# Thirty transfers of 2-byte rows on ScalarE's queue, in a decode kernel that streams a key/value cache

## The chip, the cores and the metric

The kernel runs on one core of a Trainium2 chip. The metric is the device time of one execution in microseconds (us). The kernel before took 1295.4 us (median of two runs, 1295.17 and 1295.63). A separate execution was profiled, and all rows of the trace come from it.

The engines are named as in the profile: PE is TensorE (PEld its weight loads), DVE is VectorE, ACT is ScalarE, POOL is GpSimd, SP is SyncE. A name with a q behind it (ACTq, SPq) is that engine's instruction sequencer. The core has 16 DMA engines, which carry the transfers that SP and ACT issue.

## The reference

One token per sequence (batch 8) goes through attention over a cache of 4096 positions (32 heads of 128) and, beside it, through an MLP; a sigmoid gate mixes the two.

```
q = (x @ wq) -> 8 x 32 heads x 1 x 128
p = softmax(q . k_cache / sqrt(128))        # k_cache: 8 x 32 x 4096 x 128, bf16
a = (p @ v_cache) -> 8 x 1 x 4096, @ wo     # v_cache: the same shape; wo: 4096 x 576
h = gelu(layernorm(x) @ w1 + b1)            # w1: 576 x 4608
b = h @ w2 + b2
g = sigmoid(sum(x * gate_w))
out = g * a + (1 - g) * b                   # 8 x 1 x 576
```

The two caches are 268 MB each, read once. They are nearly all of the 557 MB that the kernel moves.

## The kernel before

The work is cut into 32 groups, n = 0 to 31. A group is one sequence of the batch and 8 heads. Its keys are 8.4 MB and lie on 128 partitions (16 partitions for a head, 256 positions on each, so 64 KB per partition); its values are as large. The groups are gone through in order:

- **Scores.** `mult(n, c)` (line 501, DVE) multiplies a chunk of 32 positions by the query, which `q_group` (line 476, ACT) copied into `q_n`. PE sums the products over the 128 numbers of a head with an identity matrix (lines 512 and 183), and `reduce` (line 524, DVE) ends the sum. There are 8 chunks in a group.
- **Softmax.** DVE finds the maximum (lines 541 to 549), ACT takes the exponential (line 550), DVE writes the probabilities `P` (line 553).
- **Values.** One group behind, `pv(n - 1)` (line 565, PE) multiplies the probabilities by the values; `evict(n - 1)` (line 577, ACT) copies the sum out of PSUM into `O_sb`; `gather(n - 1)` (line 582, PE) keeps each head's own part; `norm(n - 1)` (lines 587 and 588, DVE) divides by the sum of the exponentials; `put` (line 481, ACT) stores the result.

All loads of the caches are issued by SP. `load_k(n + 1)` (line 329) waits until the first half of the keys of group n has been multiplied. `load_v(n)` (line 340) waits until `pv(n - 1)` has read the one buffer of values. Small loads go through a helper `load` (its DMA is line 288), each with a semaphore of its own; ACT issues eleven of these: `x`, `gate_w`, `b1` at the start, then `g4` (four, from the tile `stat` in SBUF to the tile `g4` in SBUF, 8 rows of 8 bytes each, after the MLP's first part), and `b2` (four of 8 rows of 288 bytes, near the end). At the end it issues one half of the output.

An engine runs its instructions in the order in which the program's text puts them on its list: what stands later in ACT's list starts after what stands earlier.

**The end.** The values of the last group come in four parts (`V_LAST`: 128, 64, 32 and 32 positions), so that the work can follow the transfers closely. `pv` takes the first two parts, `evict(last)` and `gather(last)` follow, and `pv_turned` (line 776) adds the third and the fourth part in another layout. `preset` (line 759) lays the MLP's part under the result; then come `norm_turned` (line 786), `to_rows_last` (lines 724, 710 and 730), `a_proj` (line 768, the product with `wo`, whose last rows land in pieces), two copies out of PSUM (lines 866 and 867) and two output transfers (line 871), one from SP and one from ACT. SP then waits for both to land, which ends the program.

`ident` is the 128 x 128 identity, made at the start by GpSimd (`c_id`).

Of the kernel before, what the change touches and what calls it, by code (L numbers as in the profile page):

```python
# [9 lines left out]
BF16 = mybir.dt.bfloat16  # L10
# [31 lines left out]
class Stream:  # L42
# [11 lines left out]
    def op(self, engine, fn, waits=(), dma=None, side=0):  # L54

        rec = [fn, [w for w in waits if w is not None], None, dma, (engine, side)]
        self.ops[engine].append(rec)
        if dma is not None:
            return ("dma", *dma)
        return ("op", engine, rec)  # L60
# [84 lines left out]
def bass_gated_mix__mha_block_cached__mixer_channel_mlp__decode_kernel(  # L145
# [16 lines left out]
    sb = nc.alloc_sbuf_tensor  # L162
    S = Stream(nc)
    op = S.op

    def aside(engine, fn, waits=()):
        return op(engine, fn, waits, side=1)

    def pstride(t):
        return t[tuple([slice(None)] * len(t.shape))].ap[0][0]  # L170
# [67 lines left out]
    G8 = sb("G8", [128, B], F32)  # L238
    sel_f = sb("sel_f", [128, 2, 2, 32], F32)
    O_l = sb("O_l", [128, HB], BF16)  # L240
    g4 = sb("g4", [128, 2], F32)
    ident = sb("ident", [128, 128], BF16)
    ones = sb("ones", [128, 128], F32)
# [43 lines left out]
    def load(engine, dst, src, name, waits=()):  # L287
        return op(engine, lambda e: e.dma_start(dst, src), waits, dma=(nc.alloc_semaphore(name), 16))  # L288
# [36 lines left out]
    def load_k(n):  # L325
        nK[0] += 1
        waits = [k_done[0, 1]] if n == 1 else [k_done[n - 1, k_order(n - 1)[0]], st["p_up"]]
        dst = view(KR, k_base(n), [128, NTT, DH])
        t = op("sync", lambda e: e.dma_start(dst, kv_src(A_k_cache, n)), waits, dma=(sK, 16 * nK[0]))
        k_land[n, 0] = k_land[n, 1] = t  # L330
# [5 lines left out]
    def load_v(n, t0=0, t1=NTT, waits=()):  # L336
        nV[0] += 1
        src = kv_src(A_v_cache, n)[:, t0:t1, :]
        dst = VB[:, t0:t1, :]
        t = op("sync", lambda e: e.dma_start(dst, src), [*waits, v_done.get(n - 1)], dma=(sV, 16 * nV[0]))  # L340
        v_land[n] = t
# [4 lines left out]
    v_part = []  # L346
# [18 lines left out]
    def memset(engine, ap, value):  # L365
# [3 lines left out]
    c_id = op("gpsimd", lambda e: e.affine_select(out=ident[:], in_=ident[:], compare_op=ALU.not_equal, fill=1.0,  # L369
                                                  base=0, pattern=[[-1, 128]], channel_multiplier=1), [c_id0])  # L370
# [74 lines left out]
    for half in range(2):  # L445
        for h in range(4):
            for kt in range(NKT):
                o = tr_ps[half][32 * h:32 * h + B, :]
                at = (kt * SK + half * (SK // 2) if kt < NKF else NKF * SK) + h * DH
# [14 lines left out]
    def q_of(b):  # L464
        for i in range(2):
            t = aside("tensor", lambda e, i=i: e.matmul(  # L466
                qb_ps[64 * i:64 * i + 64, :], lhsT=Sel[:, b, :],
                rhs=bass.AP(tensor=Q4, offset=i * DH, ap=[[pstride(Q4), 128], [2 * DH, NHG], [1, DH]]),
                start=True, stop=True), [*a_Q, c_Sel, a_qb.get(b - 1)] if i == 0 else ())
        a_qb[b] = aside("scalar", lambda e: e.activation(out=q_bc[:, b, :], in_=qb_ps[:, :], func=ACT.Copy), [t])  # L470
# [3 lines left out]
    def q_group(n):  # L474
        hg, b = divmod(n, B)
        a_q[n] = aside("scalar", lambda e: e.activation(out=q_n[:, :], in_=q_bc[:, b, hg * DH:(hg + 1) * DH], func=ACT.Copy),  # L476
                    [a_qb[b], v_mult.get((n - 1, NC - 1))])
# [50 lines left out]
    def scores(n, between):  # L528

        mult(n, 0)  # L530
        between(0)
        mult(n, 1)
        between(1)
        for c in range(NC):
            reduce(n, c)
            if c + 2 < NC:
                mult(n, c + 2)
                between(c + 2)
# [21 lines left out]
    def pv(n, land, t0, t1):  # L560
# [7 lines left out]
                start=(tq < 4), stop=(tq >= (NTT if n < last else T_TURN) // TQ - 4)), w)  # L568
        v_done[n] = p_pv[n]

    def total(n):
        p_z[n] = op("tensor", lambda e: e.matmul(  # L572
            oz_ps[:, HB:2 * HB], lhsT=ones[:, :], rhs=rs[:, :], start=True, stop=True),
            [v_rs[n], v_norm.get(n - 1), c_ones])
# [73 lines left out]
    def batch_rows(t, n, i):  # L648

        p = pstride(t)  # L650
        return bass.AP(tensor=t, offset=i * 32 * p, ap=[[p, B], [1, n]])
# [8 lines left out]
    def down_proj(j0, j1):  # L660
        for jt in range(j0, j1):
            st["p_down"] = quarters(hT_sb, NJ, jt, w2_sb[:, jt, :], jt == 0, jt == NJ - 1,
                                    [st["ld_w2"], st["v_h"], c_yps] if jt == 0 else (),
                                    op if jt in (j0, NJ - 1) else aside)
            st.setdefault("p_down0", st["p_down"])

    def b_out():
        st["a_bx"] = aside("scalar", lambda e: e.activation(
            out=bmg_sb[0:QP, :], in_=y_ps[0:QP, 0:QN], func=ACT.Copy), [st["p_down0"], st["p_down"]])
# [9 lines left out]
    def load_wo():  # L679

        g = H_AHEAD // HB
        st["ld_wo"] = load("sync", wo_sb[:, 0:H_AHEAD, :].rearrange("p (g r) n -> p g (r n)", g=g),
                           A_wo[0:H_AHEAD * DH, :].rearrange("(g p r) n -> p g (r n)", g=g, r=RD), "ld_wo", [k_done[last - 1, 1]])
# [96 lines left out]
    def recip(n):  # L780
        t = op("vector", lambda e: e.reciprocal(out=rz[:, :], in_=oz_ps[:, HB:2 * HB]), [p_z[n]])
        v_rz[n] = op("vector", lambda e: e.tensor_scalar(
            out=rz[:, :], in0=rz[:, :], scalar1=G8[:, n % B:n % B + 1], scalar2=None, op0=ALU.mult), [t, st["a_G8"]])
# [9 lines left out]
    for n in range(NG):  # L793
        for e, (first, turn, _) in LOOP.items():
            if n >= first and (n - first) % turn == 0:
                S.marks.setdefault(e, []).append(len(S.ops[e]))

        def between(c, n=n):
            if n == 0 and c + 1 < B:
                q_of(c + 1)  # L800

        scores(n, between)
        if n < last:
            q_group(n + 1)
            load_k(n + 1)
        if n == 0:
            load_v(0, 0, V_AHEAD, [p_Q])
            g_diag = op("gpsimd", lambda e: e.tensor_scalar(
                out=stat[:, 16:16 + B], in0=ident[0:B, 0:B], scalar1=stat[:, G_COL:G_COL + 1], scalar2=None, op0=ALU.mult), [a_g, c_id])
            t = aside("tensor", lambda e: e.matmul(oz_ps[:, 0:B], lhsT=ones[0:B, :], rhs=stat[:, 16:16 + B], start=True, stop=True),  # L810
                      [g_diag, c_ones])
            st["a_G8"] = aside("scalar", lambda e: e.activation(out=G8[:, :], in_=oz_ps[:, 0:B], func=ACT.Copy), [t])
            up_proj()
            softmax(0)
            act_h()
            c_selO = op("vector", lambda e: e.tensor_reduce(
                out=selO[:].rearrange("p t h -> p h t"),
                in_=bass.AP(tensor=ident, offset=0, ap=[[pstride(ident), 128], [TQ, HB], [1, TQ], [32, 4]]),
                axis=AX.X, op=ALU.add), [c_id])
            v_omg = op("vector", lambda e: e.tensor_scalar(out=stat[:, OMG_COL:OMG_COL + 1], in0=stat[:, G_COL:G_COL + 1],  # L820
                                                           scalar1=-1.0, scalar2=1.0, op0=ALU.mult, op1=ALU.add), [a_g, st["p_up"]])
            st["a_g4"] = a_g4 = [load("scalar", batch_rows(g4, 2, i), stat[:, G_COL:G_COL + 2], f"ld_g4{i}", [v_omg, c_g4])
                    for i in range(4)]
            down_proj(0, NJ)
            b_out()
            load_v(0, V_AHEAD, NTT, [st["p_down"]])
            continue
        if n == last - 1:
            load_wo()
        total(n - 1)  # L830
        if n == last:
            to_rows_spread(range(NHG - 1))
        pv(n - 1, v_land[n - 1], 0, NTT)
        evict(n - 1)
        gather(n - 1, oz_ps[:, 0:HB])
        if n == last:
            S.marks["tensor"].append(len(S.ops["tensor"]))
        if n < last:
            load_v(n)
        softmax(n)  # L840
        norm(n - 1)
        if n == last:
            S.marks["vector"].append(len(S.ops["vector"]))
            to_rows_spread((NHG - 1,))
            to_rows()
        if n == last - 4:
            load_b2()
            b_gate()
    load_v_last(last)
    load_wo_last()  # L850
    total(last)
    a_proj_ahead()
    recip(last)
    for i in range(2):
        pv(last, v_part[i][2], *v_part[i][:2])
    evict(last)
# [12 lines left out]
    for i, e in enumerate(("sync", "scalar")):  # L869
        half = bass.AP(tensor=out_flat.tensor, offset=out_flat.offset + i * 2 * QN, ap=[[D, B], [1, 2 * QN]])  # L870
        ld_out = op(e, lambda e, i=i, half=half: e.dma_start(half, out_sb[32 * i:32 * i + B, :]), t, dma=(s_out, 16 * (i + 1)))
    S.ops["sync"].append([lambda e: None, [ld_out], None, None, None])


    S.resolve()
# [39 lines left out]
```

## Time and profile before

| what | value |
|---|---|
| median of two runs | 1295.4 us |
| the profiled execution's own time | 1295.31 us |
| its span, first to last instruction | 1293.2 us |
| DVE busy | 852.2 us (66%) |
| PE busy | 736.9 us (57%) |
| ACT busy | 73.7 us (6%) |
| moved by DMA | 557.08 MB, 431 GB/s over the span |
| packets of SP's and ACT's queues together (q1 and q10) | 11520 and 320 |

Busy time of an engine counts its compute instructions alone: the time that a sequencer spends on issuing a DMA is not in it. A DMA's row in the timeline is that issue; the transfer itself runs later on the 16 DMA engines. A time in a timeline is counted from the start of the span; the span plus 2.1 us is the execution's own time.

### The profile page before, as it was taken

To read this page: it belongs to the slowest core of one execution; us is meant where nothing else is said; L and a number is where in the kernel's file an instruction comes from. 1 tells how busy PE (TensorE), PEld (TensorE's weight loads), DVE (VectorE), ACT (ScalarE), POOL (GpSimd) and SP (SyncE) were. 2 spreads that over 40 slices of the span, in tenths; PEclk is the share of its full clock that TensorE was granted. 3 is DMA by queue.
4 is the path that set the end of the run, shared out by engine and by line. 5 is a ranking of instruction groups with operands and counts; after the bars stand their busy time and mean duration, and the time that the engine had idled before them with its cause. 6 is when DMAs were issued, how large, how long until landed. Compare 5 with 4: busy or idle time off the path is not lost.

```text
span 1293.2 us, 11048 instructions
## 1 busy us (share of the span) xinstructions
PE 736.9 (57%) x4888; PEld 142.9 (11%) x3096; DVE 852.2 (66%) x1078; ACT 73.7 (6%) x167; POOL 13.0 (1%) x26
## 2 busy tenths in 40 slices
PE   3745566455557555556555556555556555556556
PEld 0211111011111011111011111001111001111003
DVE  3646667766667766667766667766668766667763
ACT  3300000000000000000000000000000000000001
POOL 0100000000000000000000000000000000000001
PEclk8978888777898787898778888877898787799778
DMA  9999999999999999999999999999999999999998
GB/s 406 426 447 424 428 444 428 438 434 430 444 426 428 444 428 426 444 430 438 432 430 444 426 428 444 428 430 440 430 440 432 428 444 426 428 444 428 430 434 358
DMA packets 11848, 557.08 MB, mean 431 GB/s; under 512 B 1568, under 2 KB 1728, under 8 KB 2240
## 3 DMA queue, kind: packets, MB, share of 16 engines
q1 hardware_dynamic: 11520, 556.93, 99.7%
q10 hardware_dynamic: 320, 0.04, 0.0%
q8 instruction: 5, 0.08, 0.0%
q14 instruction: 3, 0.02, 0.0%
HBM read 556.96 MB, written 0.01 MB: 431 GB/s over the span
## 4 chain that ended last, share of the span: by engine, by line
DMA 67%; DVE 18%; PE 9%; issue 4%; DVEq 1%; SPq 0%
DMA KR<-in_A_k_cache_dram 65%; DVE p L501 15%; PE psb L183 8%; DVE s_sb L524 2%; DMA KR<-in_A_wo_dram 2%; PE psb L512 2%; DVEq L524 0%; DVEq L137 0%; SPq L288 0%; PE psb L768 0%; PE psb L466 0%; DVE p L866 0%; DVEq L501 0%
## 5 line engine op out<-in xcount | busy, mean ns | idle before, releaser
L501 DVE TENSOR_TENSOR p<-KR,q_n 128x4096 bf16<-128x4096 bf16 x256 | 582.1, 2284 | 211.1 <-DMA KR<-in_A_k_cache_dram 211.1
L183 PE MATMUL psb<-p,ident 128*128 128x512 bf16 x1792 | 491.1, 420 | 0.0
L512 PE MATMUL psb<-p,ident 128*128 128x512 bf16 x256 | 112.5, 440 | 505.9 <-DVE p L501 505.9
L524 DVE TENSOR_REDUCE s_sb<-psb 128x512 f32 (+1 forms) x256 | 175.7, 686 | 109.4 <-PE psb L183 62.8
L512 PEld LDWEIGHTS psb<-p,ident 128*128 128x128 bf16 x256 | 26.5, 103 | 965.2 <-DVE p L501 964.5
L565 PE MATMUL psb<-VB,P 128*32 128x512 bf16 x1984 | 112.7, 380 | 0.0
L553 DVE TENSOR_SCALAR P<-E,own 128x256 bf16<-128x256 bf16 x256 | 53.1, 283 | 87.4 <-ACT E L550 87.4
L476 ACT ACTIVATE q_n<-q_bc 128x128 bf16<-128x128 bf16 x32 | 9.9, 309 | 873.2 <-DVE p L501 873.2
L565 PEld LDWEIGHTS psb<-VB,P 128*32 128x32 bf16 x1984 | 50.0, 97 | 48.0
L582 PE MATMUL psb<-selO,O_sb 128*128 128x8 f32 x256 | 33.9, 259 | 22.5 <-ACT O_sb L577 22.5
L582 PEld LDWEIGHTS psb<-selO,O_sb 128*128 128x128 f32 x256 | 31.0, 191 | 38.3 <-ACT O_sb L577 38.3
L577 ACT ACTIVATE O_sb<-psb 128x512 f32<-128x512 f32 x32 | 19.1, 597 | 196.8 <-PE psb L565 196.8
L572 PEld LDWEIGHTS psb<-rs,ones 128*128 128x128 f32 x64 | 12.1, 190 | 46.6 <-issue 44.4
L550 ACT ACTIVATE E<-s_sb,mD 128x256 bf16<-128x256 f32 x32 | 16.0, 499 | 0.0
L541 DVE TENSOR_REDUCE mA<-s_sb 128x1 f32<-128x256 f32 x32 | 13.4, 420 | 1.1
L481 ACT ACTIVATE OT_sb<-O_n,G 128x8 bf16<-128x8 f32 x31 | 9.3, 300 | 84.3 <-DVE O_n L588 84.3
L556 DVE TENSOR_REDUCE es<-E 128x1 f32<-128x256 bf16 x32 | 13.2, 413 | 0.0
L672 POOL TENSOR_TENSOR Q<-Q,b 104x144 f32<-104x144 f32 x1 | 0.7, 742 | 1073.9 <-DMA b<-in_B_b_dram 1073.9
L572 PE MATMUL psb<-rs,ones 128*128 128x8 f32 x64 | 9.2, 216 | 1.3 <-DVE O_n L588 1.3
L557 DVE TENSOR_SCALAR rs<-own,es 128x8 f32<-128x8 f32 x32 | 7.4, 231 | 1.1
L643 PE MATMUL psb<-VB,hT_sb 128*8 128x144 bf16 x144 | 4.5, 324 | 5.5 <-POOL hT_sb L633 5.5
L549 DVE STREAM_TRANSPOSE mD<-mC 128x32 f32<-128x32 f32 x32 | 6.8, 213 | 1.1
(97 smaller groups left out, 130.9 us busy)
## 6 DMA issues: line engine op xcount, KB each, us to landing
KR<-in_A_k_cache_dram SPq DMA_DIRECT2D x2, 4096.0 KB, 27.1
VB<-in_A_v_cache_dram SPq DMA_DIRECT2D x1, 5376.0 KB, 28.9
VB<-in_B_w_dram SPq DMA_DIRECT2D x1, 5184.0 KB, 40.5
KR<-in_B_w_dram SPq DMA_DIRECT2D x1, 4608.0 KB, 43.5
VB<-in_A_wq_dram SPq DMA_DIRECT2D x1, 4096.0 KB, 12.4
KR<-in_A_v_cache_dram SPq DMA_DIRECT2D x1, 4096.0 KB, 22.3
VB<-in_A_v_cache_dram SPq DMA_DIRECT2D x1, 2816.0 KB, 38.2
KR<-in_A_wo_dram SPq DMA_DIRECT2D x1, 2304.0 KB, 20.7
```

The costliest lines, as they stand in the source:

```text
L183: return e.add_instruction(mybir.InstMatmult(name=nc.get_next_instruction_name(), engine=mybir.EngineType.PE, ins=[e.lower_ap(rhs), e.lowe ...
L501: v_mult[n, c] = op("vector", lambda e: e.tensor_tensor(out=p1[:, par, :, :], in0=k_of(), in1=qb, op=ALU.mult), [k_land[n, s], a_q[n], p_s ...
L512: fn = lambda e, r=r: e.matmul(tr_ps[par][:, :], lhsT=ident[:, :], rhs=r, start=True, stop=False)
L524: v_red[n, c] = op("vector", lambda e: e.tensor_reduce(out=s_of(), in_=tr_ps[par][:, :].rearrange("p (t c) -> p t c", c=CH), axis=AX.X, op ...
L541: t = op("vector", lambda e: e.tensor_reduce(out=mA[:, 0:1], in_=s_sb[:, :], axis=AX.X, op=ALU.max), [v_red[n, NC - 1], c_mA])
L550: a_exp[n] = op("scalar", lambda e: e.activation(out=E[:, :], in_=s_sb[:, :], func=ACT.Exp, bias=mD[:, 0:1], scale=1.0), [v_nm[n], v_P.get ...
L553: v_P[n] = op("vector", lambda e, h=h: e.tensor_scalar(out=P[:, :, h, :], in0=E[:, :].rearrange("p (q t) -> p q t", t=TQ), scalar1=own[:, ...
L556: t = op("vector", lambda e: e.tensor_reduce(out=es[:, :], in_=E[:, :], axis=AX.X, op=ALU.add), [a_exp[n]])
L565: p_pv[n] = op("tensor", lambda e, o=o, tq=tq, at=at, v=v: e.matmul(o, lhsT=P[:, tq, :, :].rearrange("p h t -> p (h t)"), rhs=v.rearrange( ...
L572: p_z[n] = op("tensor", lambda e: e.matmul(oz_ps[:, HB:2 * HB], lhsT=ones[:, :], rhs=rs[:, :], start=True, stop=True), [v_rs[n], v_norm.ge ...
L577: a_ev[n] = op("scalar", lambda e: e.activation(out=O_sb[:].rearrange("p t d -> p (t d)"), in_=o_ps[n // last][:, :], func=ACT.Copy), [p_p ...
L582: p_oz[n] = op("tensor", lambda e, tt=tt: e.matmul(o, lhsT=O_sb[:, tt, :], rhs=selO[:, tt, :], start=(tt == 0), stop=(tt == TQ - 1 and stop)),
```

## The change

A new tile `rows_to` (128 partitions x 30 numbers of 2 bytes) is written by 30 DMAs and read by nothing. Each copies a piece of the first column of the identity: 15 rows of 2 bytes, then 14, and so on down to 1, each into a column of its own, each with a semaphore of its own. ACT issues all of them. The first set stands in group n = 2, after `q_group(3)` and `load_k(3)` and ahead of `total(1)`, `pv(1)` and `evict(1)`; it waits for `c_id`. The second set stands behind `recip(last)` and ahead of the last group's `pv` and `evict(last)`; its first transfer waits for the landing of the third part of the last group's values (`v_part[2][2]`). At the very end SP waits for all 30 semaphores beside the output's.

```diff
+    rows_to = sb("rows_to", [128, 30], BF16)
...
+    tags = []
+
+    def rows_1_to_15(name, at, waits):
+
+        for k in range(15, 0, -1):
+            tags.append(load("scalar", rows_to[0:k, at + k - 1:at + k], ident[0:k, 0:1], f"{name}{k}", [*waits, c_id] if k == 15 else ()))
...
+        if n == 2:
+            rows_1_to_15("ld_r", 0, ())
         if n == last - 1:
             load_wo()
         total(n - 1)
...
     recip(last)
+    rows_1_to_15("ld_e", 15, [v_part[2][2]])
     for i in range(2):
         pv(last, v_part[i][2], *v_part[i][:2])
     evict(last)
...
-    S.ops["sync"].append([lambda e: None, [ld_out], None, None, None])
+    S.ops["sync"].append([lambda e: None, [ld_out, *tags], None, None, None])
```

## The prediction

> **What bounds the kernel now.** I read the page first: its span, the queues, the chain.
>
> ```profile
> span 1293.2 us, 11048 instructions
> GB/s 406 426 447 424 428 444 428 438 434 430 444 426 428 444 428 426 444 430 438 432 430 444 426 428 444 428 430 440 430 440 432 428 444 426 428 444 428 430 434 358
> q1 hardware_dynamic: 11520, 556.93, 99.7%
> q10 hardware_dynamic: 320, 0.04, 0.0%
> DMA 67%; DVE 18%; PE 9%; issue 4%; DVEq 1%; SPq 0%
> ```
>
> SP's queue (q1) keeps the 16 DMA engines busy for 99.7% of the span; ACT's queue (q10) moves almost nothing. Next the windows, whose last three columns are the granted clock, the DMA share and GB/s.
>
> ```profile
> 118.31:1240.71 1122.40, 638.74 (x4002) 109.89 (x2378) 765.18 (x958) 46.44 (x116) 1.39 (x2) 0.84 1.00 433
> 118.31:157.01 38.70, 21.59 (x138) 3.78 (x82) 26.38 (x33) 1.60 (x4) 0.00 (x0) 0.85 0.99 430
> 157.01:195.72 38.71, 22.70 (x138) 3.80 (x82) 26.39 (x34) 1.60 (x4) 0.00 (x0) 0.81 1.01 437
> ```
>
> A group takes 38.70 us because its 16.8 MB take that at 433 GB/s. So in the long middle only the stream of loads counts, and an engine may be late as long as no load is issued too late. At the end the stream runs dry, and there the order of the compute engines sets the time. The change has one set of transfers in each place.
>
> **What one issue costs ACT.** Timeline rows of ACT (start, length) and the groups of line 288 (shortest, median, longest ns):
>
> ```profile
> 1.68 0.37 ACTq L288 DMA_DIRECT2D b_sb<-in_B_b_dram  x1
> 2.08 1.28 ACT L379 ACT_TABLE_LOAD   x1 [2.08 <-issue]
> ...
> 63.24 2.74 ACTq L288 DMA_DIRECT2D g<-stat  x4
> ...
> 1118.58 1.32 ACTq L288 DMA_DIRECT2D b<-in_B_b_dram  x4
> ...
> L288 ACTq DMA_DIRECT2D g<-stat x4: 632/638/732, 63.2 to 65.3; - x4
> L288 ACTq DMA_DIRECT2D b<-in_B_b_dram x4: 284/310/319, 1118.6 to 1119.6; - x4
> ```
>
> ACT's first own operation starts at 2.08, just behind the last of its three issues (1.68 + 0.37): an issue holds what stands behind it. The trace has no SBUF-to-SBUF copy of a single 2-byte number per row. The nearest row is `g4`: SBUF to SBUF too, 8 rows of 8 bytes, and 8 is also the mean of 15 to 1 rows. Its four issues start 2.1 us apart from first to last, so 0.70 us each. The lower bound is `b2`, from HBM: 1.32 / 4 = 0.33 us. For the upper bound I add the two, 1.0 us, as if an odd number of rows cost another issue. I take 0.70: 15 x 0.70 = **10.5 us** of ACT for each set (5.0 to 15).
>
> **The first set, group 2.** ACT, DVE and SP in that group, and the chain's row for the next load of keys:
>
> ```profile
> 141.67 0.31 ACT L476 ACTIVATE q_n<-q_bc 128x128 bf16<-128x128 bf16 x1 [27.37 <-DVE p L501]
> 147.33 0.60 ACT L577 ACTIVATE O_sb<-psb 128x512 f32<-128x512 f32 x1 [5.36 <-PE psb L565]
> ...
> 150.85 0.17 DVE L588 TENSOR_TENSOR O_n<-psb,rz 128x8 f32<-128x8 f32 x1
> 157.01 4.49 DVE L501 TENSOR_TENSOR p<-KR,q_n 128x4096 bf16<-128x4096 bf16 x2 [6.00 <-DMA KR<-in_A_k_cache_dram]
> ...
> 169.16 0.33 SPq L329 DMA_DIRECT2D KR<-in_A_k_cache_dram  x1
> ...
> 169.16 26.34 DMA KR<-in_A_k_cache_dram
> ```
>
> The 15 issues start behind `q_n` at 141.7 and end at 152.2. Queued behind them are `evict(1)`, the exponential of group 2 and `put(1)`; PE's gather and DVE's `P` and `norm(1)` wait for those. `evict(1)` started at 147.33, so all of them come 4.9 us late. DVE had 6.00 us of idle time before the next keys, which hides it. Behind that stands a second cover: the keys issued at 169.16 land after 26.34 us, while 8.4 MB at 433 GB/s take 19.4; they queue for 7.0 us, by which their issue could slip. SP's issues do not stand in ACT's queue, and the load of the values waits for `pv(1)`, which is ahead of `evict(1)`. Cost: **0**. Without either cover it would be 4.9 us.
>
> **What the transfers take from the DMA engines.** ACT's queue in the 20 us after `g4` (62 to 82), and the period in which `b2` was drained:
>
> ```profile
> q10 hardware_dynamic: 64, 0.00, 0.2%
> ...
> 1124.55:1163.31 38.76, 21.92 (x138) 3.78 (x82) 26.52 (x34) 1.60 (x4) 1.39 (x2) 0.85 1.01 435
> ```
>
> Four transfers of 8 rows made 64 packets: two for a row, data and most likely its semaphore. They took 0.2% of 16 x 20 us, 0.01 us each. If each row goes to an engine of its own, the busiest engine gets 30 packets of a set: 0.3 us, 0.6 for both. `b2` made as many packets and its period is 0.06 us longer, or 0.2 us for 30 packets. At the end the loads will no longer be what is waited for, so I take **0** (bound 0.6).
>
> **The second set, at the end.** The landing of the last two value parts (issued at 1264.4 and 1264.9) and the timeline behind it:
>
> ```profile
> L288 SPq DMA_DIRECT2D KR<-in_A_v_cache_dram x2: 429/431/433, 1264.4 to 1264.9; - x2
> DMA to landing us min/median/max: 18.1/19.1/20.1
> ...
> 1281.19 0.60 ACT L577 ACTIVATE O_sb<-psb 128x512 f32<-128x512 f32 x1 [1.54 <-PE psb L565]
> 1281.84 1.06 PE L582 MATMUL psb<-selO,O_sb 128*128 128x8 f32 x8 [0.70 <-ACT O_sb L577]
> 1282.76 0.94 PE L776 MATMUL psb<-P,KR 128*128 128x8 bf16 x32
> 1283.63 0.45 PE L759 MATMUL psb<-Q,sel_f 104*40 104x144 f32 x4
> 1285.06 1.01 PE L776 MATMUL psb<-P,KR 128*128 128x8 bf16 x32 [0.99 <-DMA KR<-in_A_v_cache_dram]
> 1286.12 0.17 DVE L786 TENSOR_TENSOR O_l<-psb,rz 128x8 bf16<-128x8 f32 x1 [11.13 <-PE psb L776]
> ...
> 1289.56 1.36 PE L768 MATMUL psb<-KR,OT_sb 128*8 128x144 bf16 x32 [0.46 <-DMA KR<-in_A_wo_dram]
> ```
>
> The third part lands at 1264.4 + 18.1 = 1282.5. Only then does ACT begin to issue; 10.5 us later, at 1293.0, comes `evict(last)`, which ran at 1281.19 before. Behind it on ACT stand only the copy of line 867 and half the output, but the whole rest waits for it: gather, both `pv_turned` (in PE's order behind gather), the norm, `a_proj`, the output. From the start of the eviction to line 786 it was 1286.12 - 1281.19 = 4.93, of which 0.99 was a wait for the fourth part, long landed by then: 3.94. From there to the end of the span 7.08, of which 0.46 was a wait for `wo`: 6.62.
>
> PE will have idled for some 12 us, and it comes back slow after such a wait:
>
> ```profile
> 1243.46 3.19 PE L183 MATMUL psb<-p,ident 128*128 128x512 bf16 x7
> ...
> 1250.31 1.67 PE L183 MATMUL psb<-p,ident 128*128 128x512 bf16 x7
> ...
> 1243.06:1246.25 3.19, 3.19 (x8) 0.25 (x2) 2.14 (x1) 0.00 (x0) 0.00 (x0) 0.50 1.21 520
> ```
>
> Right behind an idle stretch the granted clock is 0.50 and seven multiplications take 3.19 us instead of 1.67. The gather, the first `pv_turned` and the preset ran 1281.84 to 1284.08, 2.24 us. At that ratio they lose 0.91 x 2.24 = 2.0; if loads and issue bound them, nothing. They have 8 or 144 columns, not 512, so I take **0.7**. The Trainium skill ("TensorE: Matmul & The Clock Gate", Part 1, on the clock gate) says that an idle window of about 3.4 us halves the clock until PE has been busy for about as long. By that alone everything up to the output's product would double, and the sum would come out at about 1308.7; the trace agrees on the half clock.
>
> Last, SP now passes 30 more semaphores after the output has landed. Two such waits on POOL's queue (17 ns each):
>
> ```profile
> L884 POOLq EVENT_SEMAPHORE  x2: 17/17/17, 1293.0 to 1293.1; - x2
> ```
>
> 30 x 0.017 = 0.5 us, or about 0.08 apart, 2.3; I take **1.0**.
>
> **The sum.** 1293.0 + 3.94 + 0.7 + 6.62 + 1.0 = 1305.3 for the span, against 1293.2. The profiled execution took 1295.31, 2.1 more than its span and 0.1 from the median of 1295.4: **1307.4 us**, 0.9% slower. With 0.33 us an issue it is 1301.9, with 1.0 it is 1311.9; the other two terms move it by 0.7 down or 1.3 up each.
>
> **The rivals.**
>
> *ACT's queue is full (slower by far).* A row's two packets wait each for a 64 KB packet of SP's queue on its engine, 2.42 us at 433 / 16 GB/s. Draining 30 takes 73 us. If the queue took only the 8 per engine that `g4` shows, ACT would stand for 22 x 2.42 = 53 us in group 2, until 195; `evict(1)` would be 47.6 late, less 6.0 and 7.0 of cover: 34.6, so 1342 us. It costs something from a capacity of 22 downwards (a stall of 18.6 us, past both covers), and over 2% from 16 downwards. Against it stand SP's first issues and the landing of the last large one:
>
> ```profile
> 0.74 0.88 SPq L288 DMA_DIRECT2D VB<-in_A_wq_dram  x2
> 1.67 1.20 SPq L288 DMA_DIRECT2D KR<-in_A_k_cache_dram  x2
> 2.91 0.97 SPq L288 DMA_DIRECT2D KR<-in_B_w_dram  x2
> ...
> KR<-in_B_w_dram SPq DMA_DIRECT2D x1, 4608.0 KB, 43.5
> ```
>
> Six transfers of 128 rows, 8 rows and a semaphore for each engine, 54 in all, were taken within 3.9 us, although the work lasted 43.5. The Trainium skill ("Perfetto Trace Analysis", Per-instruction lifecycle) speaks of a descriptor buffer that can fill while a sequencer issues; no row here shows one filling.
>
> *The issues do not hold ACT (no change).* The eviction would then come at 1282.5, 1.3 late. Of this 0.99 goes into the wait for the fourth part and the rest into that for `wo`; 1.0 for the semaphores is left: 1296.4. The table load at 2.08 speaks against it.
>
> *The engines get out of step and stream faster (the other side).* The busiest engine is delayed the most, so the 16 would be spread apart from group 2 on. Over the 1099 us from 141.7 to 1240.7 the rate would have to rise from 433 to 437.8 GB/s to pay for the 12.1 us; at the best slice's 447 it saves 34.4, which makes 1273. For it: slices from 424 to 447. Against it: neighbouring periods show 430 and 437 with a share of 0.99 and 1.01, so it is counting by packets, and the engines are never idle. The Trainium skill ("DMA: Bandwidth & Descriptors", Latency and other measured facts) reports losses when the rows of lock-stepped streams lie a large power of two apart, as an inference about HBM channels; the loss would show as a low rate, and the trace shows none.
>
> *Nothing is issued,* as no one reads the tile: 1295.4.
>
> **How the numbers follow.** The forecast, late eviction by issues of 0.33 to 1.0 us, has 0.86; a full queue 0.05, issues that hold nothing 0.04, nothing issued 0.03, a faster stream 0.02. The range 1300.5 to 1312.5 holds the bounds of the issue and a little of the smaller terms; outside are the other four and some 0.05 of the forecast's own. A difference of 2%, 26 us, is about what a measurement of this kernel can tell from no change: faster 0.01, within it 0.94, slower 0.05.
>
> **What would show it.** Right: 15 issues on ACT from 141.7 and from 1282.5, about 0.7 us each; `evict(1)` near 152 with the next keys still at 157.0; periods of 38.70 throughout; `evict(last)` near 1293, a granted clock of 0.50 behind it, no wait for loads from there on. Wrong: an eviction at 1282.5, issues in group 2 of microseconds each, keys of group 3 that DVE takes later than 157.0, or periods other than 38.7.

## The result and the profile after

| | median | ratio to before, 95% interval |
|---|---|---|
| before | 1295.40 us | |
| changed | 1307.24 us (1307.15 to 1307.32, two runs) | 1.0091 [1.0075, 1.0107] |

The changed kernel is 11.8 us (0.9%) slower, within the 2% that the prediction called about no change. The forecast was 1307.4. Its profiled execution took 1307.32 us.

First the page of the changed kernel (span, queues, shares of the chain that ended last), then two of its windows.

```profile
span 1305.5 us, 11093 instructions
...
q1 hardware_dynamic: 11520, 556.93, 98.7%
q10 hardware_dynamic: 800, 0.04, 0.0%
...
DMA 64%; DVE 18%; PE 9%; issue 5%; ACTq 2%; DVEq 1%; ACT 0%; SPq 0%
```

```profile
157.01:195.72 38.71, 21.81 (x138) 3.78 (x82) 26.43 (x34) 1.90 (x5) 0.00 (x0) 0.85 1.00 432
...
118.31:1240.71 1122.40, 634.26 (x4002) 110.47 (x2378) 764.80 (x957) 46.48 (x116) 4.97 (x2) 0.84 1.00 433
```

The same 1122.4 us run at the same 433 GB/s. ACT's queue has 480 packets more, two for each of the 240 rows, and SP's queue still fills the engines until its last loads have landed. New in the chain is ACTq with 2%: ACT's sequencer, issuing.

Group 2, in the timelines of ACT and of DVE:

```profile
141.80 11.54 ACTq L289 DMA_DIRECT2D rows_to<-ident  x15
153.39 0.60 ACT L585 ACTIVATE O_sb<-psb 128x512 f32<-128x512 f32 x1 [11.28 <-issue]
...
156.90 0.17 DVE L596 TENSOR_TENSOR O_n<-psb,rz 128x8 f32<-128x8 f32 x1
157.47 4.49 DVE L502 TENSOR_TENSOR p<-KR,q_n 128x4096 bf16<-128x4096 bf16 x2 [0.41 <-issue]
```

`evict(1)` (now line 585) comes 6.1 us later than before. DVE's idle time ahead of the next keys, 6.00 us before, is gone: it no longer waits for the keys but comes 0.41 us behind its own work, 0.46 us late. The prediction had named keys taken later than 157.0 as a sign of being wrong. Here it is the edge of the first cover: the load that hangs on these keys is issued 0.46 us later too (169.62 for 169.16), within the second cover, and the next group starts 0.27 late (195.99 for 195.72).

The end, all engines:

```profile
1282.97 11.26 ACTq L289 DMA_DIRECT2D rows_to<-ident  x15
1294.27 0.60 ACT L585 ACTIVATE O_sb<-psb 128x512 f32<-128x512 f32 x1 [13.96 <-issue]
...
1294.92 1.88 PE L590 MATMUL psb<-selO,O_sb 128*128 128x8 f32 x8 [12.64 <-ACT O_sb L585]
...
1296.65 0.99 PE L784 MATMUL psb<-P,KR 128*128 128x8 bf16 x32
...
1299.27 0.17 DVE L794 TENSOR_TENSOR O_l<-psb,rz 128x8 bf16<-128x8 f32 x1 [23.86 <-PE psb L784]
...
1301.11 2.10 PE L776 MATMUL psb<-KR,OT_sb 128*8 128x144 bf16 x64 [0.53 <-DVE OT_sb L738]
...
1303.64 0.32 ACTq L882 DMA_DIRECT2D out_dram<-p  x1
```

The last eviction is shown with 13.96 us of idle time that ended with "issue", which says that the profile names nothing that it waited for; its sequencer was issuing. It starts 13.08 us later than before (1.78 until the value part has landed, 11.3 of issues). To the norm's line it takes 5.00 us instead of 4.93: the wait for the fourth part is gone, the gather has grown from 1.06 to 1.88. From there to the end it takes 6.23 instead of 7.08, since no product waits for `wo` any more (64 in one run of 2.10 us). 13.08 + 0.07 - 0.85 = 12.3, which is the difference of the spans.

### The profile page after: what moved, and what is told of

The parts are those of the page before. It is cut to its first block, busy times and chain, and to the rows that moved or that the text cites. A ratio compares the mean times of both kernels' runs of the same rounds, so it can differ in the third digit from the quotient of the medians.

```text
span 1305.5 us, 11093 instructions
## 1 busy us (share of the span) xinstructions
PE 732.6 (56%) x4888; PEld 145.0 (11%) x3096; DVE 851.4 (65%) x1078; ACT 73.8 (6%) x167; POOL 16.5 (1%) x26
## 4 chain that ended last, share of the span: by engine, by line
DMA 64%; DVE 18%; PE 9%; issue 5%; ACTq 2%; DVEq 1%; ACT 0%; SPq 0%
DMA KR<-in_A_k_cache_dram 63%; DVE p L502 16%; PE psb L183 7%; DVE s_sb L525 3%; ACTq L289 2%; PE psb L513 1%; DMA KR<-in_A_v_cache_dram 1%; DVEq L525 0%; DVEq L137 0%; PE psb L776 0%; PE psb L590 0%; PE psb L784 0%; DVE P L554 0%; ACT O_sb L585 0%; SPq L289 0%
## 5 line engine op out<-in xcount | busy, mean ns | idle before, releaser
L183 PE MATMUL psb<-p,ident 128*128 128x512 bf16 x1792 | 485.6, 416 | 0.0
L513 PE MATMUL psb<-p,ident 128*128 128x512 bf16 x256 | 112.0, 437 | 506.4 <-DVE p L502 506.2
L580 PEld LDWEIGHTS psb<-rs,ones 128*128 128x128 f32 x64 | 12.3, 194 | 46.6 <-issue 44.4
L544 DVE STREAM_TRANSPOSE mB<-mA 128x32 f32<-128x32 f32 x32 | 6.8, 212 | 1.1
```

The lines of the kernel that those rows point to most:

```text
L183: return e.add_instruction(mybir.InstMatmult(name=nc.get_next_instruction_name(), engine=mybir.EngineType.PE, ins=[e.lower_ap(rhs), e.lowe ...
L513: fn = lambda e, r=r: e.matmul(tr_ps[par][:, :], lhsT=ident[:, :], rhs=r, start=True, stop=False)
L580: p_z[n] = op("tensor", lambda e: e.matmul(oz_ps[:, HB:2 * HB], lhsT=ones[:, :], rhs=rs[:, :], start=True, stop=True), [v_rs[n], v_norm.ge ...
```

## Experiments

All times are medians; each ratio is against runs of the kernel before in the same session (1295.28 to 1295.39 us).

**Each set alone.** The edits leave out one of the two calls.

```diff
 # first set alone
-    rows_1_to_15("ld_e", 15, [v_part[2][2]])
 # second set alone
-        if n == 2:
-            rows_1_to_15("ld_r", 0, ())
```

> The first set alone (group 2), without the second. Theory (the second set makes the loss, the first is hidden by DVE's wait for the keys): at most 0.4 us over before, about 1295.8 us, periods of 38.70 us, the last keys land within 0.5 us of before, the end like that of before. Rival (the transfers disturb the stream of loads, each set costs about half): some 6 us over before, about 1301, with periods longer than 38.70 behind group 2. Rival (engines out of step stream faster): below 1294.

Measured: 1295.13 us, ratio 1.0000 [0.9991, 1.0009]. ACT is held as long as in the changed kernel (first row: in group 2), and the last eviction (second row) is where it was:

```profile
141.50 11.52 ACTq L289 DMA_DIRECT2D rows_to<-ident  x15
...
1281.32 0.60 ACT L585 ACTIVATE O_sb<-psb 128x512 f32<-128x512 f32 x1 [1.52 <-PE psb L566]
```

> The second set alone. Theory: the third value part lands at 1282.5, 15 issues of 0.75 us end at 1293.8, the last eviction starts there and the rest takes 11.2 us to the end of the span, 1305.0; with 2 us around the span 1306.9 us, 11.5 over before. Rival (each set costs about half): about 1301.

Measured: 1307.17 us, ratio 1.0091 [1.0076, 1.0107], the changed kernel's own. So the second set is the whole loss, and 11.5 us of a held ACT in the middle cost nothing. Both rivals on the stream fall: it is neither disturbed nor made faster.

**The same transfers, behind the eviction.**

```diff
-    rows_1_to_15("ld_e", 15, [v_part[2][2]])
     for i in range(2):
         pv(last, v_part[i][2], *v_part[i][:2])
     evict(last)
+    rows_1_to_15("ld_e", 15, [v_part[2][2]])
```

> The second set alone, moved behind the last eviction in ACT's list; nothing else changed. Theory (the loss is what stands behind the issues on ACT, not the transfers): the last eviction at 1281.2 as before, the issues still from 1282.5 to 1293.8; behind them only the copy out of PSUM that before started at 1290.97 and half the output: the copy starts 2.9 us late, the time is 1298.2 us, 2.9 over before. Rival (the 15 transfers themselves delay the landing of the last loads or the compute): it stays near 1306.9.

Measured: 1298.27 us, ratio 1.0024 [1.0014, 1.0033]. Timeline of ACT:

```profile
1281.22 0.60 ACT L585 ACTIVATE O_sb<-psb 128x512 f32<-128x512 f32 x1 [1.77 <-PE psb L566]
1282.58 11.59 ACTq L289 DMA_DIRECT2D rows_to<-ident  x15
1294.22 0.29 ACT L876 ACTIVATE p<-psb 40x144 bf16<-40x144 f32 x1 [12.40 <-issue]
```

The same issues at the same time now hold only the last copy, 3.2 us over its time of before, and the loss is 3.0 us. Of the 11.9, 8.9 hung on the eviction alone. The transfers as such cost nothing that can be seen.

**What makes an issue dear.** Two runs of the second set alone: from HBM instead of SBUF, and with 8 rows each.

```diff
 # from HBM
-  load("scalar", rows_to[0:k, at + k - 1:at + k], ident[0:k, 0:1], ...)
+  src = bass.AP(tensor=A_wo.tensor, offset=A_wo.offset, ap=[[D, k], [1, 1]])
+  e.dma_start(rows_to[0:k, at + k - 1:at + k], src, ...)
 # eight rows
+  load("scalar", rows_to[0:8, at + k - 1:at + k], ident[0:8, 0:1], ...)
```

> The second set alone, with rows of 2 bytes from HBM (the first column of wo, a row of 1152 bytes apart) in place of the identity in SBUF; same row counts, same tile written. Theory (an issue is dear because both ends are in SBUF, as in the four copies of g4): 0.33 us each as for b2, 5.0 us for the set, last eviction at 1287.5, time about 1300.6 us. Rival (it is the short rows or the row counts): 0.75 us each as from SBUF, about 1306.9.

> The second set alone, all 15 transfers of 8 rows (120 rows as before), instead of 15 to 1. Theory (an SBUF-to-SBUF issue costs some 0.65 us, and row counts that are odd or large add to it): 0.67 us each as for the one transfer of 8 rows in the set, 10.4 us with gaps instead of 11.7, time about 1305.8 us against 1307.2. Rival (row counts do not matter): 1307.2.

Measured: 1301.31 us, ratio 1.0046 [1.0032, 1.0060], and 1305.80 us, ratio 1.0081 [1.0065, 1.0096]. Shortest, median and longest issue in ns: in the changed kernel (both sets), from HBM, and with 8 rows:

```profile
L289 ACTq DMA_DIRECT2D rows_to<-ident x30: 607/730/917, 141.8 to 1293.6; - x30
```

```profile
L578 ACTq DMA_DIRECT2D rows_to<-in_A_wo_dram x15: 263/318/402, 1282.7 to 1288.1; - x15
```

```profile
L289 ACTq DMA_DIRECT2D rows_to<-ident x15: 631/631/649, 1282.5 to 1292.1; - x15
```

With the same short rows and row counts, HBM as the source takes 0.32 us where SBUF takes 0.73. With 8 rows it is 0.63 throughout, as for the 8 rows of `g4`; so it is the two ends in SBUF that make it dear (the output, from SBUF to HBM, takes 0.32 us on ACT in the rows of the end above), and row counts add to it.

**Without the wait for the value part.**

```diff
-    rows_1_to_15("ld_e", 15, [v_part[2][2]])
+    rows_1_to_15("ld_e", 15, ())
```

> The second set alone, without its wait for the third value part (it starts when ACT is done with the copies of line 752). Theory: the same 11.7 us of issues from about 1279.5, last eviction at 1291.2, time 1304.1 us, 3.1 below that of the second set with the wait. Rival (the landing of the loads holds the rest anyway): 1307.2.

Measured: 1302.79 us, ratio 1.0058 [1.0041, 1.0075]: 4.4 us below the set with its wait, more than the 3.1 expected. The timeline of ACT shows why:

```profile
1278.06 0.28 ACT L752 ACTIVATE p<-psb 32x144 f32<-32x144 f32 x1 [3.54 <-PE psb L748]
1278.07 0.87 ACTq L289 DMA_DIRECT2D rows_to<-ident  x1
1278.35 0.87 ACT L752 ACTIVATE p<-psb 32x144 f32<-32x144 f32 x3
```

The sequencer issues the first transfer while the four copies ahead of it still run; I had let it start behind them. An issue holds what stands behind it, not what has already been handed to the engine.

**PE kept busy.** 58 products into an unused bank ahead of the last gather, in the second set alone.

```diff
     evict(last)
+    for i in range(58):
+        aside("tensor", lambda e: e.matmul(o_ps[0][:, :], lhsT=ident[:, :], rhs=Sel[:].rearrange("p b r -> p (b r)"), start=True, stop=True), ...)
     gather(last, qb_ps[:, 0:HB], False)
```

> The second set alone, and 58 more matrix products (128 x 512, into a bank that nobody reads any more) on PE ahead of the last gather, so that PE is busy while ACT issues. Theory (PE's half clock behind its idle stretch costs about 1.1 us between the last eviction and line 794's norm): gather back from 1.9 to about 1.06 us, time 1.1 to 1.5 us below that of the second set alone, about 1305.9. Rival (the half clock costs nothing there): 1307.2.

Measured: 1306.57 us, ratio 1.0086 [1.0071, 1.0101]. From the start of the last eviction to the norm's line, first for the second set alone and then with PE kept busy (the third number from the end is the granted clock), and the gather of the latter:

```profile
1294.31:1299.31 5.00, 4.31 (x76) 3.78 (x76) 0.00 (x1) 0.60 (x1) 0.00 (x0) 0.50 0.01 3
```

```profile
1294.77:1298.58 3.81, 3.12 (x76) 2.79 (x76) 0.00 (x1) 0.59 (x1) 0.00 (x0) 1.00 0.00 0
```

```profile
1295.41 1.06 PE L590 MATMUL psb<-selO,O_sb 128*128 128x8 f32 x8 [1.58 <-ACT O_sb L585]
```

At the full clock the stretch takes 3.81 us instead of 5.00, so the half clock costs 1.2. The total gained only 0.6, because the eviction came 0.46 us later in that profile: the same issues took 12.10 us instead of 11.69, one of them 1.28 us, where the longest of the second set alone took 0.88. What stretched it is open.

**The second set where nobody waits.** On SP's list, behind the last load of `wo`, without the wait; the first set as it was.

```diff
     load_wo_last()
+    rows_1_to_15("ld_e", 15, (), "sync")
...
-    rows_1_to_15("ld_e", 15, [v_part[2][2]])
```

> Both sets, the second on SP's list behind the last load of wo and without the wait for the value part; SP has nothing else to do there. Theory (a place where nothing waits behind the issues makes them free): issues on SP from 1267.5 to about 1279, last eviction at 1281.2, time 1295.4 us within 0.6, the 15 transfers landing at about 1291 to 1292 behind the last loads. Rival (the transfers sit ahead of SP's half of the output in its queue and hold it, or the wait for them ends last): 1297 or more.

Measured: 1295.75 us, ratio 1.0004 [0.9995, 1.0013]. All 30 transfers are made, at no cost that can be told from none. But the issues on SP took longer than expected:

```profile
L289 SPq DMA_DIRECT2D rows_to<-ident x15: 597/722/3481, 1267.7 to 1282.3; - x15
```

One took 3.48 us. SP had just issued eight large loads there, so a full queue, which the prediction thought unlikely for ACT, was worth a test of its own.

**The first set enlarged: both covers, and the queue.** Thirty transfers in group 2, and sixty of one row each; none at the end.

```diff
 # thirty
             rows_1_to_15("ld_r", 0, ())
+            rows_1_to_15("ld_s", 15, ())
 # sixty
+            for j in range(60):
+                load("scalar", rows_to[j // 30:j // 30 + 1, j % 30:j % 30 + 1], ident[0:1, 0:1], ...)
```

> Thirty transfers in group 2 (the first set twice, in other columns), none at the end. The first set alone left DVE starting the next keys 0.4 us behind the end of its own work, so the first cover of 6.0 us is just used up. Theory (behind it stands a second cover, the 7.0 us by which the next keys wait in SP's queue): ACT issues until 164.6, DVE takes the keys of group 3 at about 168.7, the load of the keys of group 4 is issued 11.5 us late, of which 7.0 are covered: 4.3 us over before, about 1299.6 us, once, with periods of 38.70 behind it. Rival (no second cover): 11.5 over, about 1306.8. Rival (a queue that is full beyond some 16 transfers): issues of microseconds each and well over 1307.

Measured: 1303.41 us, ratio 1.0061 [1.0048, 1.0075]: 8.0 us over before, between theory (4.3) and the rival without a second cover (11.5). Timeline of SP, a window (its last two numbers are the DMA share and GB/s) and the chain:

```profile
180.57 0.33 SPq L330 DMA_DIRECT2D KR<-in_A_k_cache_dram  x1
```

```profile
176.00:180.50 4.50, 2.00 (x9) 0.10 (x1) 4.50 (x4) 0.00 (x0) 0.00 (x0) 1.00 0.00 0
```

```profile
180.57 22.04 DMA KR<-in_A_k_cache_dram
...
1221.34 26.35 DMA KR<-in_A_k_cache_dram
...
1273.04 24.75 DMA KR<-in_A_wo_dram
```

The keys of group 4 are issued 11.4 us late, as expected. The stream had run dry by 176.0: the window from there on shows no bytes. So the second cover was there, 6.8 us of the 7.0, and 4.5 went uncovered. But the load then took 22.04 us to land, where 8.4 MB take 19.4 at the stream's rate: starting an empty stream cost 2.7 more. From there the period is the old one, and the last keys land at 1247.7 instead of 1240.5, 7.2 late, which is the 4.5 and the 2.7. The load of `wo` lands 8.3 late (1297.8 against 1289.5); the last 1.1 arises between the two and is not explained.

> Sixty transfers of one row in group 2, none at the end; one row goes to one DMA engine, so that engine's part of ACT's queue gets 120 packets. Theory (the queue holds a limited number of packets per engine, about 70, as two long issues on SP in the run with the set on SP suggest): about 40 issues of 0.62 us, from then on one transfer per two 64 KB packets, 4.8 us each; ACT free only near 264 us, time some 1400 us. Rival (no limit within 120 packets): all issues at 0.62 us, ACT free at 180, the eviction 33 us late, less 13.0 of cover, and 3.8 for the restart and the end as in the run with thirty: about 1319 us.

Measured: 1324.30 us, ratio 1.0223 [1.0206, 1.0240]. The group of the issues, three stretches of ACT's timeline, then what ACT's queue had moved from 141 until 164.77:

```profile
L289 ACTq DMA_DIRECT2D rows_to<-ident x60: 562/564/2411, 141.8 to 184.0; - x60
```

```profile
141.79 22.94 ACTq L289 DMA_DIRECT2D rows_to<-ident  x38
...
164.77 6.92 ACTq L289 DMA_DIRECT2D rows_to<-ident  x3
...
172.31 2.18 ACTq L289 DMA_DIRECT2D rows_to<-ident  x1
```

```profile
q10 hardware_dynamic: 9, 0.00, 0.0%
```

The first 38 issues take 0.56 us each, 22.94 us with what lies between them. Then come three long ones, 6.92 us together, the longest of 2.4 us, about the time of a 64 KB packet, and after one short issue a fourth of 2.18. By 164.77, 76 packets had been handed over and 9 moved: the queue held some 67. They sat before one DMA engine, as far as their pace shows it: three more moved by 171.9, one for each 64 KB packet's time. So there is a limit, as theory said. But the 60 issues took 42.8 us in all, about 7 more than at 0.59 each, and theory's 1400 us falls. The trace shows why: SP's queue ran dry. From 174.2 to 174.6, first both queues (ACT's is q10), then a window from 174.2 to 199:

```profile
q10 hardware_dynamic: 64, 0.00, 10.2%
q1 hardware_dynamic: 3, 0.00, 0.4%
```

```profile
174.20:199.00 24.80, 9.18 (x29) 2.13 (x11) 10.84 (x18) 1.29 (x3) 0.00 (x0) 0.55 0.00 0
```

The last values had landed, and the next keys were issued only at 200.86, for that issue waits until DVE has multiplied keys of group 3, and DVE stood behind ACT. With no 64 KB packets left to wait for, 64 of ACT's packets moved within 0.4 us, and every later issue is short again. Theory had let the stream run on while ACT stood. With ACT's eviction at 184.6, 37.3 late, less 13.0 of cover, plus the 3.8 seen in the run with thirty, the sum is 28.1; measured were 28.9.

## Why the prediction was right

**The place of the loss.** Right, and shown by the runs with one set alone and by the set moved behind the eviction.

**An issue's cost.** 0.70 us, taken from `g4`; measured 11.26 us for 15, 0.75 (0.78 in the run of the second set alone, 11.69 us). The choice of the nearest row was right, and its reason too (the run from HBM would have been the lower bound, 0.32 to 0.38 with gaps). The argument that 8 rows stand for the mean of 15 to 1 was a little off: 8 rows take 0.63, the longest issue 0.92.

**The first set.** Right in its result, with less to spare than thought: the eviction was 6.1 us late and not 4.9, which used up the first cover of 6.00 and left DVE 0.46 us late, by the prediction's own list a sign of being wrong. That this cost nothing is due to the second cover, which the prediction had behind the first. The second cover exists but is worth less than its 7.0 us once it is overrun, for the empty stream has to start again.

**The start of the second set.** 1282.97 for 1282.5. In the run of the second set alone it was 1282.57; in the profile of the changed kernel all of SP's last loads are issued 0.4 us later than before (the last keys at 1214.57 for 1214.14), and the value part with them.

**PE's clock.** 0.7 was taken between 0 and 2.0; the runs give 1.1 to 1.2. The gather, in f32, nearly doubles (1.06 to 1.88); the products of line 784, whose 32 weight loads take about as long as they do, hardly change (0.94 to 0.99). The Trainium skill ("TensorE: Matmul & The Clock Gate", Part 1) says that the clock stays high only while PE is busy; the run with the 58 products agrees, granted clock 1.00 for 0.50. Its doubling, taken for every product, would have been too much. The 1308.7 that the prediction gives for it counts the gather, the first `pv_turned` and the preset alone; the second `pv_turned` (1.01) would add up to 0.9. It did not grow (1.01 in the changed kernel too). Behind the norm nothing could grow by the clock, for there it stood at 0.50 already in the kernel before (third number from the end):

```profile
1286.12:1291.00 4.88, 3.11 (x72) 1.99 (x72) 1.07 (x4) 0.03 (x1) 0.00 (x0) 0.50 0.62 241
```

**The rest of the chain.** 6.62 us to the end of the span, measured 6.23: more of the wait for `wo` went than the one of 0.46 that I took off, since the smaller ones behind it went too.

**The semaphores at the end.** This term was wrong: 1.0 us was taken, about nothing was measured. SP's waits:

```profile
L99 SPq EVENT_SEMAPHORE  x16: 17/28/28, 1303.6 to 1304.9; - x16
```

All fall between the issue of the output at 1303.64 and the end at 1305.5. From that issue to the end it takes 1.9 us, exactly as before: the waits lie beside the output's flight. I had put them behind it. (The lower bound of this term was 0.5, so it could move the sum by 0.5 down, and not by the 0.7 that the prediction gives for both terms.)

So the sum was off by +0.8 for the issues, +0.5 for the start, +0.4 for the clock, -0.4 for the chain and -1.0 for the semaphores, which nearly cancel in the span (1305.3 for 1305.5). The 2.1 us that were added for the execution's own time came out as 1.8. That the forecast lies within 0.2 us is partly luck.

**The transfers themselves.** 0 was taken, with 0.6 as the bound: nothing was measured. The first set alone is not slower than before, and behind the eviction the loss is no more than the last copy's delay.

**The rivals.** Issues that do not hold ACT: refuted by ACT's rows in every run. Nothing issued: refuted by the 480 packets more. A faster stream: refuted by the first set alone (1295.13) and the same 433 GB/s. A full queue: real, at about 67 packets of one-row transfers, but the first set, by the prediction's count, puts 30 on the busiest engine, and thirty transfers (60 packets, some of them moved meanwhile) still found room, with no issue above 0.91 us. The Trainium skill ("Perfetto Trace Analysis", Per-instruction lifecycle) speaks of a descriptor buffer that fills up; the run with sixty shows issues growing from 0.56 to 2.4 us, which agrees with it, though the trace does not name what they wait for.

## What to carry to other kernels

A DMA issue is work of the engine that issues it, 0.3 us or more than twice that, and no row of busy time shows it: count what stands behind it in that engine's list. Hidden issues are bought from the idle time that another engine had; measure that cover in its own row and ask what happens when it is overrun, since a stream that has run dry costs more than the gap itself. At the end of a kernel there is no cover, and the same instructions go on a list, or to a place on it, behind which nobody waits.

## What the runs showed of the hardware

- An issue with both ends in SBUF took 0.56 us for one row, 0.63 for 8 rows and up to 0.92 for 15, with the source in HBM 0.32 (medians of 0.73 and 0.32 for the same 15 to 1 rows).
- ACT's queue took some 67 packets of one-row transfers, which moved one per 2.4 us beside SP's stream, before an issue had to wait, up to 2.4 us. Once SP's queue was empty, 64 of them moved within 0.4 us.
- A load of 8.4 MB that found the queues empty landed 22.0 us after its issue, instead of the 19.4 that its bytes take at the stream's 433 GB/s.
